# Row-form loads with 28 to 32 KB packets for the output, gate, up and down projections of a decode block on one Trainium2 core

## The chip, the cores and the metric

The kernel is a program for one core of a Trainium2 chip. The metric is device time in microseconds (us). Timed runs of the two kernels alternate on the same chip ("rounds"), and the profiled execution gives a trace. A ratio below is the mean time of one kernel's fast runs over that of the other's of the same rounds, so it is not quite the ratio of the medians that stand beside it; with it comes a 95% interval. The later sessions ran on three different chips (12, 9 and 3 in the record), so a run is compared with the kernel before of its own rounds unless the text says otherwise.

## The reference, cut to what matters

One decode step (sequence length 1) for a batch of 8: adaptive layer norm, grouped-query attention over a long cache, a ReGLU feed-forward block. Everything is bf16.

```python
# x (8,1,1024); k_cache, v_cache (8,4,8192,128): 67 MB each; wq (1024,4096); wo (4096,1024)
# W_gate, W_up (1024,3584); W_down (3584,1024); w_mod (1024,6144)
mod = silu(c) @ w_mod                      # six vectors: sa, ca, ga, sb, cb, gb
h = layernorm(x) * (1 + ca) + sa
x = x + ga * (attention(h @ wq, k_cache, v_cache) @ wo)      # 32 heads, 4 KV heads
h = layernorm(x) * (1 + cb) + sb
x = x + gb * ((relu(h @ W_gate) * (h @ W_up)) @ W_down)
```

185.6 MB are read from HBM once each and used for 8 rows, so the kernel is a stream of loads with computation hung onto it. K and V are 134.2 MB of it, wo 8.4 MB, gate and up 14.7 MB together, W_down 7.3 MB.

## The kernel before

All large loads go through one ring in SBUF, `arena`: nine slots of 8192 bf16 elements per partition. A load is issued by SP, the engine that only issues DMAs, as soon as everything in its target space has been read (`pump`). Loads start in order, and a load of 128 partitions is spread over the core's 16 DMA engines, 8 partitions each: a K or V load lands 4.9 us after the one before it, which is eight packets of 611 ns.

The loads that the change touches. What matters is the contiguous run in HBM that goes to one partition, because it becomes one DMA packet (the trace of the kernel before has 4096 packets of 2 KB for wo): for wo, eight runs of 2 KB per partition and load; for gate and up, 14 KB; for W_down, 14 KB.

```python
wo_src = A_wo.rearrange("(q h d) n -> q d h n", q=4, d=128)      # partition = element d of a head
g_src = B_W_gate.rearrange("(p k) n -> p (k n)", k=KC)
u_src = B_W_up.rearrange("(p k) n -> p (k n)", k=KC)
d_src = B_W_down.rearrange("(q p r) n -> q p (r n)", p=128, r=FR)   # FR = 7
for i in range(4):
    load(("wo", i), wo_src[i], SLOT)
for i in range(4):
    load(("gate", i), g_src[:, i * 2 * F:(i + 1) * 2 * F], 2 * F)
    load(("up", i), u_src[:, i * 2 * F:(i + 1) * 2 * F], 2 * F)
wd_parts = [(q, 0, FR) for q in range(NB - 1)] + [(NB - 1, 0, 4), (NB - 1, 4, 6), (NB - 1, 6, 7)]
for i, (q, r0, r1) in enumerate(wd_parts):
    load(("wd", i), d_src[q][:, r0 * D:r1 * D], (r1 - r0) * D)
```

Attention works on 32 groups (8 batch entries x 4 KV heads). For our argument one part matters: the product of the probabilities with V takes 64 small matmuls per group, each with its own weight load.

```python
def pv(n):
    z = n % 2
    col = n * J
    # ... (vv: V of the group as 64 chunks of 128 keys; pv_: the probabilities, turned)
    for cc in range(NC):                          # NC = 64
        fns.append(lambda e, cc=cc: e.matmul(ps[:, 3, col:col + J], vv[:, cc, :], pv_[:, cc % 16, cc // 16, :],
                                             start=(cc == 0), stop=(cc == NC - 1)))
```

The four projections of the tail: wo with oT (128 elements of a head x 32 heads) as it comes out of attention; gate and up with the weights as the stationary operand, 28 blocks of 128 outputs; W_down column-tiled, four column tiles of 32 each for a quarter of the outputs.

```python
# wo: 32 heads x 4 column tiles, moving 256 columns
ps[32 * j:32 * j + 32, 5, 0:256], oT[:, h, :], w[:, hh, j, :]
# gate, up: per row block kk, 28 matmuls of 8 moving columns, each with a 128x128 weight load
ps[:, 0, off + f * B:off + (f + 1) * B], w[:, f // FR, f % FR, :], hT[:, kk, 0:B]
# ... relu and product on 128x224, written as hmT for W_down
```

Of the kernel before, what the change touches and what calls it, by code (L numbers as in the profile page):

```python
# [132 lines left out]
def bass_adaLN_cond__gqa_block_cached__glu_gated_reglu__decode_kernel(nc, A_x, A_k_cache, A_v_cache, A_wq, A_wo, B_x, B_W_gate, B_W_up, B_W_down, c, w_mod, out):  # L133
# [13 lines left out]
    FR = 7  # L147
    NB = F // (128 * FR)
    KF = NB * FR

    P = Prog()
    with ExitStack() as es:
        E = es.enter_context

        def sb(name, shape, dtype):
            return E(nc.sbuf_tensor(name, shape, dtype))
# [34 lines left out]
        grel = sb("grel", [128, KF, B], dt.float32)  # L191
        hmT = sb("hmT", [128, KF, 32], dt.bfloat16)
# [7 lines left out]
        def R(t, lo=0, hi=1):  # L200
            return (t, lo, hi)
# [4 lines left out]
        def slot_r(lo, hi):  # L206
            return ("arena", lo, hi)
# [5 lines left out]
        def load(key, src, n):  # L213
            stream.append((key, src, n))
# [17 lines left out]
        wo_src = A_wo.rearrange("(q h d) n -> q d h n", q=4, d=128)  # L232
        g_src = B_W_gate.rearrange("(p k) n -> p (k n)", k=KC)
        u_src = B_W_up.rearrange("(p k) n -> p (k n)", k=KC)
        d_src = B_W_down.rearrange("(q p r) n -> q p (r n)", p=128, r=FR)
# [7 lines left out]
        for i in range(4):  # L243
            load(("wo", i), wo_src[i], SLOT)
        for i in range(4):
            load(("gate", i), g_src[:, i * 2 * F:(i + 1) * 2 * F], 2 * F)
            load(("up", i), u_src[:, i * 2 * F:(i + 1) * 2 * F], 2 * F)
        wd_parts = [(q, 0, FR) for q in range(NB - 1)] + [(NB - 1, 0, 4), (NB - 1, 4, 6), (NB - 1, 6, 7)]
        for i, (q, r0, r1) in enumerate(wd_parts):
            load(("wd", i), d_src[q][:, r0 * D:r1 * D], (r1 - r0) * D)  # L250
# [23 lines left out]
        P.op("pool", lambda e: e.memset(hmT[:], 0.0), writes=[R("hmT", 0, KF)])  # L274
# [228 lines left out]
        for q in range(4):  # L503
            w = arena[:, place["wo", q]:place["wo", q] + SLOT].rearrange("p (h j n) -> p h j n", h=8, j=4)
            fns = []
            for hh in range(8):
                for j in range(4):
                    h = 8 * q + hh
                    fns.append(lambda e, w=w, hh=hh, h=h, j=j: e.matmul(  # L509
                        ps[32 * j:32 * j + 32, 5, 0:256], oT[:, h, :], w[:, hh, j, :], start=(h == 0), stop=(h == Hq - 1),  # L510
                        tile_position=(0, 32 * j)))
            P.op("pe", fns, reads=[R("oT"), slot_r(place["wo", q], place["wo", q] + SLOT)], writes=[bank(5)])
# [8 lines left out]
        for i in range(4):  # L521
            gf, uf = [], []
            for kk in (2 * i, 2 * i + 1):
                for fns, base, off in ((gf, place["gate", i], 0), (uf, place["up", i], KF * B)):
                    w = arena[:, base + (kk % 2) * F:base + (kk % 2 + 1) * F].rearrange("p (q x r) -> p q r x", q=NB, r=FR)
                    for f in range(KF):
                        first = kk == 0 and off == 0 and f == 0
                        fns.append(lambda e, w=w, f=f, kk=kk, off=off, first=first: e.matmul(  # L528
                            ps[:, 0, off + f * B:off + (f + 1) * B], w[:, f // FR, f % FR, :], hT[:, kk, 0:B],
                            start=first, stop=(kk == KC - 1), skip_group_check=True))  # L530
            P.op("pe", gf, reads=[R("hT"), slot_r(place["gate", i], place["gate", i] + 2 * F)], writes=[bank(0)])
            P.op("pe", uf, reads=[R("hT"), slot_r(place["up", i], place["up", i] + 2 * F)], writes=[bank(0)])
        P.op("act", lambda e: e.activation(grel[:].rearrange("p f b -> p (f b)"), ps[:, 0, 0:KF * B], ACT.Relu),  # L533
             reads=[bank(0)], writes=[R("grel")])
        P.op("dve", lambda e: e.tensor_tensor(out=hmT[:, :, 0:B], in0=ps[:, 0, KF * B:2 * KF * B].rearrange("p (f b) -> p f b", b=B),  # L535
                                              in1=grel[:], op=ALU.mult),
             reads=[bank(0), R("grel"), R("hmT", 0, KF)], writes=[R("hmT", 0, KF)])
        for i, (q, r0, r1) in enumerate(wd_parts):
            lo, hi = place["wd", i], place["wd", i] + (r1 - r0) * D
            w = arena[:, lo:hi].rearrange("p (r j n) -> p r j n", r=r1 - r0, j=4)  # L540
            fns = []
            for r in range(r0, r1):
                for j in range(4):
                    f = q * FR + r
                    fns.append(lambda e, w=w, r=r - r0, f=f, j=j: e.matmul(  # L545
                        ps[32 * j:32 * j + 32, 1, 0:256], hmT[:, f, :], w[:, r, j, :], start=(f == 0), stop=(f == KF - 1),
                        tile_position=(0, 32 * j)))
            P.op("pe", fns, reads=[R("hmT", 0, KF), slot_r(lo, hi)], writes=[bank(1)])
        P.op("dve", lambda e: e.tensor_tensor(out=lu[:], in0=ps[:, 1, 0:256], in1=mod[:, 5, :], op=ALU.mult),
             reads=[bank(1), R("mod", 5, 6)], writes=[R("lu")])  # L550
# [45 lines left out]
```

## Time and profile before

| | before |
|---|---|
| time, median of 4 runs | 445.77 us (445.73 to 446.13) |
| span of the traced run | 444.1 us |
| bytes read from HBM | 185.63 MB |
| DMA packets | 16,770 |
| PE, DVE busy | 66%, 49% |

The DMA part of the page of the kernel before. The line "DMA" has one digit per fortieth of the span, the mean busy share of the 16 DMA engines in tenths (9 is 90% or more), and "GB/s" what they moved. Queue q1 carries the kernel's loads; q8 and q14 carry instructions to the core's engines.

```profile
DMA  8999999999999999999999999999999999999993
GB/s 344 421 428 425 434 434 428 426 429 437 427 428 432 431 426 426 435 434 425 426 434 429 425 429 435 429 425 432 429 430 428 429 421 403 422 430 429 426 429 151
DMA packets 16770, 186.14 MB, mean 419 GB/s; under 512 B 1537, under 2 KB 1633, under 8 KB 5985
...
q1 hardware_dynamic: 16704, 185.64, 98.5%
q8 instruction: 27, 0.44, 0.4%
...
DMA 83%; PE 8%; DVE 7%; issue 1%; ACT 0%; SPq 0%; POOL 0%; DVEq 0%; ACTq 0%; POOLq 0%
```

The reader should see three things. The DMA engines are busy from the second slice on, and the last line, the chain of work that ended last, is DMA for 83% of its length: the kernel is bound by its stream of loads. There is a dip to 403 GB/s in the slice from 366 to 377 us, which is where wo begins to arrive. And the last slice is at 151 GB/s.

The table of stretches for the tail, kernel before. Columns: stretch in us, its length, busy time (and number of instructions) of PE, PE's weight loads, DVE, ACT and POOL, granted PE clock, DMA share (busy packet time over 16 engines' time), GB/s.

```profile
core 0: us, PE busy (x) PEld busy (x) DVE busy (x) ACT busy (x) POOL busy (x), PEclk, DMA share, GB/s
300.00:366.00 66.00, 48.64 (x566) 26.15 (x565) 40.54 (x60) 5.44 (x14) 4.05 (x20) 0.82 1.01 428
366.00:388.00 22.00, 14.25 (x255) 10.25 (x251) 7.87 (x15) 2.84 (x5) 0.00 (x0) 0.77 1.05 411
388.00:421.00 33.00, 22.97 (x413) 22.20 (x414) 4.33 (x11) 0.20 (x1) 0.00 (x0) 0.53 1.01 429
...
431.00:436.00 5.00, 1.69 (x28) 0.96 (x28) 0.00 (x0) 0.00 (x0) 0.00 (x0) 0.50 0.90 377
436.00:440.00 4.00, 2.97 (x52) 1.52 (x52) 0.00 (x0) 0.00 (x0) 0.00 (x0) 0.50 0.41 167
```

In wo's stretch (366 to 388 us) the DMA share is 1.05. In the last two rows the share falls to 0.90 and 0.41 while loads are still outstanding: some of the 16 engines have finished and others have not.

PE's own waits after 366 us, kernel before, longest first (engine, tile and line; what it waited for; us in total, times, longest):

```profile
PE ps L545 <- DMA arena<-in_B_W_down_dram: 7.4, 5, 2.9
PE ps L528 <- DMA arena<-in_B_W_up_dram: 3.0, 3, 1.4
PE ps L509 <- DMA arena<-in_A_wo_dram: 2.6, 1, 2.6
...
PE ps L528 <- DMA arena<-in_B_W_gate_dram: 2.3, 2, 1.2
```

PE waits 15.3 us for loads in the tail, so work taken from it there cannot shorten the kernel by itself.

The reading of the last two stretches can be made exact. A load's semaphore is incremented once by each of its 16 engines when that engine's share has landed. The skill says the same ("DMA: Bandwidth & Descriptors", "Why a DMA increments its semaphore by 16 and not by 1": only the full 16 means that all data landed), and the trace records the times of the increments. For the last load of W_down in the kernel before (first of the 16 landings at 434.43 us of the span), the others came after it by, in us:

```
0.00 0.11 0.72 0.95 1.23 1.40 1.42 3.12 4.18 4.19 4.54 5.28 5.42 5.59 5.60 5.91
```

The kernel cannot go on before the last of them, at 440.33 us. I call the distance from the first to the last landing of this load the lag; it is 5.9 us here. For the fourth load of wq, at 52 us, it was 1.5 us, and for the last load of w_mod, at 32 us, 1.2 us.

### The profile page before, as it was taken

The page shows a single profiled execution, that of the slowest core. Times are in us where ns is not written, and L with a number is a line of the kernel's source. Part 1 is how long each engine was busy: PE and PEld are TensorE (multiplying, and loading weights), DVE is VectorE, ACT ScalarE, POOL GpSimd, SP SyncE. Part 2 cuts the span into 40 slices and gives each one's busy share as a digit, 9 for nine tenths or more (in the row PEclk, how much of TensorE's full clock was granted, in tenths as well). Part 3 has the DMA queues.
Part 4 walks back from the last instruction along what each step waited for, and adds up shares of the span by engine and source line. Part 5 has one row for each costly group of instructions (what it writes and reads, how often), then busy time and mean ns, then how long its engine had stood idle before and what let it go on. Part 6 is the DMA issues. An engine that isn't in the chain of part 4 may idle for free.

```text
span 444.1 us, 7822 instructions
## 1 busy us (share of the span) xinstructions
PE 290.9 (66%) x3514; PEld 165.4 (37%) x3514; DVE 217.7 (49%) x333; ACT 33.2 (7%) x78; POOL 30.8 (7%) x141
## 2 busy tenths in 40 slices
PE   0235355677858676776877767786777787558753
PEld 0111022344434333443433334343333345348741
DVE  0503065666655566666555566665556664230000
ACT  0200010000001000000100000001000002000000
POOL 4000020100000001000000110000001000000000
PEclk9995576887788888879688888778888869655555
DMA  8999999999999999999999999999999999999993
GB/s 344 421 428 425 434 434 428 426 429 437 427 428 432 431 426 426 435 434 425 426 434 429 425 429 435 429 425 432 429 430 428 429 421 403 422 430 429 426 429 151
DMA packets 16770, 186.14 MB, mean 419 GB/s; under 512 B 1537, under 2 KB 1633, under 8 KB 5985
## 3 DMA queue, kind: packets, MB, share of 16 engines
q1 hardware_dynamic: 16704, 185.64, 98.5%
q8 instruction: 27, 0.44, 0.4%
q14 instruction: 7, 0.05, 0.0%
q10 hardware_dynamic: 32, 0.01, 0.0%
HBM read 185.63 MB, written 0.02 MB: 418 GB/s over the span
## 4 chain that ended last, share of the span: by engine, by line
DMA 83%; PE 8%; DVE 7%; issue 1%; ACT 0%; SPq 0%; POOL 0%; DVEq 0%; ACTq 0%; POOLq 0%
DMA arena<-in_A_k_cache_dram 62%; DMA arena<-in_B_W_down_dram 8%; DMA arena<-in_A_wq_dram 7%; DMA arena<-in_A_wo_dram 4%; PE ps L460 4%; DVE kt L411 3%; DMA c_r<-in_c_dram 2%; PE ps L528 1%; DVE pT L450 1%; PE ps L334 1%; PE ps L420 1%; PE ps L357 0%; DVE lu L281 0%; ACT L278 0%; DVE hT L286 0%
## 5 line engine op out<-in xcount | busy, mean ns | idle before, releaser
L411 DVE STREAM_TRANSPOSE kt<-arena 128x1024 uint32<-128x1024 uint32 x128 | 153.3, 1218 | 114.6 <-DMA arena<-in_A_k_cache_dram 114.6
L420 PE MATMUL ps<-kt,qpad 128*128 128x512 bf16 x512 | 161.5, 482 | 2.0 <-POOL qpad L400 2.0
L420 PEld LDWEIGHTS ps<-kt,qpad 128*128 128x128 bf16 x512 | 60.9, 119 | 91.8 <-issue 60.6
L460 PE MATMUL ps<-pT,arena 128*128 128x8 bf16 x2048 | 56.0, 166 | 49.2 <-DVE pT L450 49.2
L460 PEld LDWEIGHTS ps<-pT,arena 128*128 128x128 bf16 x2048 | 54.1, 96 | 63.6 <-issue 63.3
L400 POOL COPY qpad<-qR 32x32 bf16<-32x32 bf16 x128 | 26.0, 203 | 312.8 <-PE ps L420 256.0
L430 PE MATMUL ps<-identf,negm 128*128 128x128 f32 x64 | 20.2, 408 | 37.0 <-DVE negm L426 37.0
L444 ACT ACTIVATE prb<-ps,bias 128x512 bf16<-128x512 f32 x32 | 22.0, 687 | 283.9 <-DVE mjt L438 283.9
L528 PE MATMUL ps<-hT,arena 128*128 128x8 bf16 x448 | 24.8, 194 | 7.7 <-DMA arena<-in_B_W_up_dram 3.0
L528 PEld LDWEIGHTS ps<-hT,arena 128*128 128x128 bf16 x448 | 24.4, 153 | 8.1 <-DMA arena<-in_B_W_up_dram 3.2
L430 PEld LDWEIGHTS ps<-identf,negm 128*128 128x128 f32 x64 | 12.3, 240 | 40.3 <-DVE negm L426 40.3
L450 DVE STREAM_TRANSPOSE pT<-prb 128x512 bf16<-128x512 bf16 x32 | 21.5, 672 | 1.7 <-ACT prb L444 1.7
L426 DVE TENSOR_REDUCE negm<-ps 128x1 f32<-128x512 f32 x32 | 20.9, 653 | 1.0 <-PE ps L420 1.0
L535 DVE TENSOR_TENSOR hmT<-ps,grel 128x224 bf16<-128x224 f32 x1 | 0.4, 391 | 30.7 <-ACT grel L533 30.7
L357 PE MATMUL ps<-arena,hT 128*32 128x512 bf16 x64 | 7.6, 627 | 11.2 <-DMA arena<-in_A_wq_dram 8.4
L303 PE MATMUL ps<-st,sel 128*128 128x1 f32 x4 | 1.2, 362 | 19.3 <-DVE st L302 19.3
L334 PE MATMUL ps<-arena,hT 128*32 128x512 bf16 x96 | 9.0, 544 | 6.8 <-DMA arena<-in_w_mod_dram 6.8
L545 PE MATMUL ps<-arena,hmT 128*32 128x256 bf16 x112 | 7.1, 415 | 7.4 <-DMA arena<-in_B_W_down_dram 7.4
L509 PE MATMUL ps<-arena,oT 128*32 128x256 bf16 x128 | 6.4, 382 | 5.2 <-DMA arena<-in_A_wo_dram 2.6
L341 DVE COPY mod<-ps 128x512 f32<-128x512 f32 x2 | 1.3, 670 | 15.2 <-PE ps L334 15.2
L436 DVE TENSOR_REDUCE mj<-ps 128x8 f32<-128x128 f32 x32 | 8.1, 252 | 1.2 <-PE ps L430 1.2
L303 PEld LDWEIGHTS ps<-st,sel 128*128 128x128 f32 x4 | 1.0, 310 | 19.6 <-DVE st L302 19.6
(64 smaller groups left out, 66.0 us busy)
## 6 DMA issues: line engine op xcount, KB each, us to landing
arena<-in_A_k_cache_dram SPq DMA_DIRECT2D x32, 2048.0 KB, 25.7
arena<-in_A_v_cache_dram SPq DMA_DIRECT2D x32, 2048.0 KB, 30.2
arena<-in_w_mod_dram SPq DMA_DIRECT2D x4, 3072.0 KB, 18.2
arena<-in_A_wq_dram SPq DMA_DIRECT2D x4, 2048.0 KB, 35.0
arena<-in_A_wo_dram SPq DMA_DIRECT2D x4, 2048.0 KB, 19.1
arena<-in_B_W_gate_dram SPq DMA_DIRECT2D x4, 1792.0 KB, 24.2
arena<-in_B_W_up_dram SPq DMA_DIRECT2D x4, 1792.0 KB, 28.0
arena<-in_B_W_down_dram SPq DMA_DIRECT2D x3, 1792.0 KB, 33.8
```

What stands on the lines that cost most here:

```text
L334: fns.append(lambda e, w=w, pr=pr, j=j, kk=kk: e.matmul(ps[32 * j:32 * j + 32, pr, :], hT[:, kk, :], w[:, 2 * pr:2 * pr + 2, j, :], start= ...
L357: fns.append(lambda e, w=w, z=z, g=g, kk=kk: e.matmul(ps[32 * g:32 * g + 32, 3 + z, :], hT[:, kk, :], w[:, g, z, :], start=(kk == 0), stop ...
L400: P.op("pool", lambda e, n=n, Q=Q: e.tensor_copy(qpad[32 * Q:32 * Q + 32, n % NQ, :, 24 + 32 * Q:32 + 32 * Q], qR[32 * Q:32 * Q + 32, :, n ...
L411: P.op("dve", lambda e: e.transpose(ktb[:, to:to + QE].bitcast(dt.uint32), arena[:, lo:lo + QE].bitcast(dt.uint32)), reads=[slot_r(lo, lo ...
L420: fns.append(lambda e, t=t, r=r: e.matmul(ps[:, n % 2, :].rearrange("p (c k) -> p c k", k=32), qpad[:, n % NQ, t * 2 + r, 24 - 8 * i:152 - ...
L426: P.op("dve", lambda e: e.tensor_reduce(negm[:, n % 2:n % 2 + 1], ps[:, n % 2, :], AX.X, ALU.max, negate=True), reads=[bank(n % 2)], write ...
L430: P.op("pe", lambda e: e.matmul(ps[:, 2, 0:128], negm[:, n % 2:n % 2 + 1].to_broadcast([128, 128]), identf[:], start=True, stop=True), rea ...
L436: P.op("dve", lambda e: e.tensor_reduce(mj[:, z, :], ps[:, 2, 0:128].rearrange("p (m j) -> p j m", j=J), AX.X, ALU.min), reads=[bank(2)], ...
L444: P.op("act", lambda e: e.activation(prb[:, z, :], ps[:, z, :], ACT.Exp, bias=bias[:, z:z + 1], scale=scale, accum_out=lall[:, n:n + 1]), ...
L450: P.op("dve", lambda e: e.transpose(pT[:, z, :], prb[:, z, :]), reads=[R("prb", z, z + 1)], writes=[R("pT", z, z + 1)])
L460: fns.append(lambda e, cc=cc: e.matmul(ps[:, 3, col:col + J], vv[:, cc, :], pv_[:, cc % 16, cc // 16, :], start=(cc == 0), stop=(cc == NC ...
L528: fns.append(lambda e, w=w, f=f, kk=kk, off=off, first=first: e.matmul(ps[:, 0, off + f * B:off + (f + 1) * B], w[:, f // FR, f % FR, :], ...
```

## The change

Its intent is to give every weight of the tail the form "partition p holds consecutive rows", so that each partition receives long contiguous runs: wo in two loads of 32 KB per partition instead of four with 2 KB runs, gate and up in two loads each of 28 KB, W_down in parts of 28, 14, 8, 4 and 2 KB. For that the activations need the matching row order, which costs work: the heads are turned into rows by 32 small matmuls with an identity, two evacuations and one DVE transpose. Gate and up swap their operands: activations become stationary, weights move, and four column tiles work side by side (the Trainium skill's "TensorEngine Tiling (Array Packing)", "When to Use Tiling", names this "Stationary-Streaming Swap + Column Tiling"). That leaves 128 matmuls where there were 448.

```diff
-        wo_src = A_wo.rearrange("(q h d) n -> q d h n", q=4, d=128)
+        wo_src = A_wo.rearrange("(p k) n -> p (k n)", k=KO)
-        d_src = B_W_down.rearrange("(q p r) n -> q p (r n)", p=128, r=FR)
+        d_src = B_W_down.rearrange("(p k) n -> p (k n)", k=KF)
-        for i in range(4):
-            load(("wo", i), wo_src[i], SLOT)
 ...
+        wo_parts = [(0, 16), (16, 32)]
+        for i, (r0, r1) in enumerate(wo_parts):
+            load(("wo", i), wo_src[:, r0 * D:r1 * D], (r1 - r0) * D)
+        gu_parts = [(0, 4), (4, 8)]
+        for i, (r0, r1) in enumerate(gu_parts):
+            load(("gate", i), g_src[:, r0 * F:r1 * F], (r1 - r0) * F)
+            load(("up", i), u_src[:, r0 * F:r1 * F], (r1 - r0) * F)
+        wd_parts = [(0, 14), (14, 21), (21, 25), (25, 27), (27, 28)]
 ...
+        for z in range(2):                       # heads into rows
+            for jj in range(4):
+                for g in range(G):
+                    ... e.matmul(ps[32 * g:32 * g + 32, z, 128 * jj:128 * jj + 128], oT[:, J * g + 4 * z + jj, :], identb[:], ...
 ...
+        P.op("dve", lambda e: e.transpose(oX, orow... .rearrange("p (x k) -> p k x", k=KO)), ...
 ...
-                            ps[:, 0, off + f * B:off + (f + 1) * B], w[:, f // FR, f % FR, :], hT[:, kk, 0:B],
+                                ps[32 * j:32 * j + 32, b0 + h, 0:H], hT[:, kk, :], w[:, r, j, h, :],
+                                start=(kk == 0), stop=(kk == KC - 1), tile_position=(0, 32 * j)))
 ...
+        P.op("dve", lambda e: e.transpose(hmT, hrow.rearrange("p (x k) -> p k x", k=KF)), ...
```

Some small tiles move into space of the K buffer that is free by then.

More of the change, by code (lines that the diff above doesn't have):

```diff
@@ L146, in bass_adaLN_cond__gqa_block_cached__glu_gated_reglu__decode_kernel @@
     NSLOT = 9
-    FR = 7
-    NB = F // (128 * FR)
-    KF = NB * FR
+    KF = F // 128
+    KO = Hq * Dh // 128
+    FJ = F // 4
     P = Prog()
@@ L190, in bass_adaLN_cond__gqa_block_cached__glu_gated_reglu__decode_kernel @@
         oT = sb("oT", [128, Hq, 32], dt.bfloat16)
-        grel = sb("grel", [128, KF, B], dt.float32)
-        hmT = sb("hmT", [128, KF, 32], dt.bfloat16)
+        orow = ktb[:, 0:1024].rearrange("p (j d) -> p j d", j=J)
+        oX = ktb[:, 1024:2048].rearrange("p (k b) -> p k b", b=32)
+        hrow = ktb[:, 2048:2048 + FJ]
+        hmT = ktb[:, 3072:3072 + FJ].rearrange("p (k b) -> p k b", b=32)
+        grel = ktb[:, 4096:4096 + 2 * FJ].bitcast(dt.float32)
+        r_oX, r_hmT = ("kt", 1024, 2048), ("kt", 3072, 4096)
         ob = sb("ob", [128, 256], dt.bfloat16)
@@ L242, in bass_adaLN_cond__gqa_block_cached__glu_gated_reglu__decode_kernel @@
             load(("v", n), A_v_cache[n // G, n % G].rearrange("(p c) d -> p (c d)", p=128), SLOT)
-        for i in range(4):
-            load(("wo", i), wo_src[i], SLOT)
-        for i in range(4):
-            load(("gate", i), g_src[:, i * 2 * F:(i + 1) * 2 * F], 2 * F)
-            load(("up", i), u_src[:, i * 2 * F:(i + 1) * 2 * F], 2 * F)
-        wd_parts = [(q, 0, FR) for q in range(NB - 1)] + [(NB - 1, 0, 4), (NB - 1, 4, 6), (NB - 1, 6, 7)]
-        for i, (q, r0, r1) in enumerate(wd_parts):
-            load(("wd", i), d_src[q][:, r0 * D:r1 * D], (r1 - r0) * D)
+        wo_parts = [(0, 16), (16, 32)]
[6 more added lines that the diff above has]
+        wd_parts = [(0, 14), (14, 21), (21, 25), (25, 27), (27, 28)]
+        for i, (r0, r1) in enumerate(wd_parts):
+            load(("wd", i), d_src[:, r0 * D:r1 * D], (r1 - r0) * D)
         P.op("pool", lambda e: e.memset(c_r[:], 0.0), writes=[R("c_r", 0, 4)])
@@ L273, in bass_adaLN_cond__gqa_block_cached__glu_gated_reglu__decode_kernel @@
         P.op("pool", lambda e: e.memset(oT[:], 0.0), writes=[R("oT")])
-        P.op("pool", lambda e: e.memset(hmT[:], 0.0), writes=[R("hmT", 0, KF)])
         P.op("pool", lambda e: e.tensor_copy(identb[:], identf[:]), reads=[R("identf")], writes=[R("identb")])
@@ L500, in bass_adaLN_cond__gqa_block_cached__glu_gated_reglu__decode_kernel @@
              reads=[bank(3), R("lx"), R("oT")], writes=[R("oT")])
-        for q in range(4):
-            w = arena[:, place["wo", q]:place["wo", q] + SLOT].rearrange("p (h j n) -> p h j n", h=8, j=4)
+        for z in range(2):
             fns = []
-            for hh in range(8):
+            for jj in range(4):
+                for g in range(G):
+                    fns.append(lambda e, z=z, jj=jj, g=g: e.matmul(
+                        ps[32 * g:32 * g + 32, z, 128 * jj:128 * jj + 128], oT[:, J * g + 4 * z + jj, :], identb[:],
+                        start=True, stop=True, tile_position=(0, 32 * g)))
+            P.op("pe", fns, reads=[R("oT"), R("identb")], writes=[bank(z)])
+            dst = orow[:, 4 * z:4 * z + 4, :].rearrange("p j d -> p (j d)")
+            if z == 0:
+                P.op("dve", lambda e, dst=dst, z=z: e.tensor_copy(dst, ps[:, z, :]), reads=[bank(z)], writes=[("kt", 512 * z, 512 * z + 512)])
+            else:
+                P.op("act", lambda e, dst=dst, z=z: e.activation(dst, ps[:, z, :], ACT.Copy), reads=[bank(z)],
+                     writes=[("kt", 512 * z, 512 * z + 512)])
+        P.op("dve", lambda e: e.transpose(oX, orow.rearrange("p j d -> p (j d)").rearrange("p (x k) -> p k x", k=KO)),
+             reads=[("kt", 0, 1024)], writes=[r_oX])
+        for i, (r0, r1) in enumerate(wo_parts):
+            lo, hi = place["wo", i], place["wo", i] + (r1 - r0) * D
+            w = arena[:, lo:hi].rearrange("p (r j n) -> p r j n", r=r1 - r0, j=4)
+            fns = []
+            for k in range(r0, r1):
                 for j in range(4):
-                    h = 8 * q + hh
-                    fns.append(lambda e, w=w, hh=hh, h=h, j=j: e.matmul(
-                        ps[32 * j:32 * j + 32, 5, 0:256], oT[:, h, :], w[:, hh, j, :], start=(h == 0), stop=(h == Hq - 1),
+                    fns.append(lambda e, w=w, r=k - r0, k=k, j=j: e.matmul(
+                        ps[32 * j:32 * j + 32, 5, 0:256], oX[:, k, :], w[:, r, j, :], start=(k == 0), stop=(k == KO - 1),
                         tile_position=(0, 32 * j)))
-            P.op("pe", fns, reads=[R("oT"), slot_r(place["wo", q], place["wo", q] + SLOT)], writes=[bank(5)])
+            P.op("pe", fns, reads=[r_oX, slot_r(lo, hi)], writes=[bank(5)])
         P.op("dve", lambda e: e.tensor_tensor(out=lu[:], in0=ps[:, 5, 0:256], in1=mod[:, 2, :], op=ALU.mult),
@@ L518, in bass_adaLN_cond__gqa_block_cached__glu_gated_reglu__decode_kernel @@
         modulate(4, 3)
-        for i in range(4):
-            gf, uf = [], []
-            for kk in (2 * i, 2 * i + 1):
-                for fns, base, off in ((gf, place["gate", i], 0), (uf, place["up", i], KF * B)):
-                    w = arena[:, base + (kk % 2) * F:base + (kk % 2 + 1) * F].rearrange("p (q x r) -> p q r x", q=NB, r=FR)
-                    for f in range(KF):
-                        first = kk == 0 and off == 0 and f == 0
-                        fns.append(lambda e, w=w, f=f, kk=kk, off=off, first=first: e.matmul(
-                            ps[:, 0, off + f * B:off + (f + 1) * B], w[:, f // FR, f % FR, :], hT[:, kk, 0:B],
-                            start=first, stop=(kk == KC - 1), skip_group_check=True))
-            P.op("pe", gf, reads=[R("hT"), slot_r(place["gate", i], place["gate", i] + 2 * F)], writes=[bank(0)])
-            P.op("pe", uf, reads=[R("hT"), slot_r(place["up", i], place["up", i] + 2 * F)], writes=[bank(0)])
@@ L533, in bass_adaLN_cond__gqa_block_cached__glu_gated_reglu__decode_kernel @@
-        P.op("act", lambda e: e.activation(grel[:].rearrange("p f b -> p (f b)"), ps[:, 0, 0:KF * B], ACT.Relu),
-             reads=[bank(0)], writes=[R("grel")])
-        P.op("dve", lambda e: e.tensor_tensor(out=hmT[:, :, 0:B], in0=ps[:, 0, KF * B:2 * KF * B].rearrange("p (f b) -> p f b", b=B),
-                                              in1=grel[:], op=ALU.mult),
-             reads=[bank(0), R("grel"), R("hmT", 0, KF)], writes=[R("hmT", 0, KF)])
-        for i, (q, r0, r1) in enumerate(wd_parts):
+        H = FJ // 2
@@ new lines, in bass_adaLN_cond__gqa_block_cached__glu_gated_reglu__decode_kernel @@
+        for i, (r0, r1) in enumerate(gu_parts):
+            for nm, b0 in (("gate", 0), ("up", 2)):
+                lo, hi = place[nm, i], place[nm, i] + (r1 - r0) * F
+                w = arena[:, lo:hi].rearrange("p (r j h n) -> p r j h n", r=r1 - r0, j=4, h=2)
+                fns = []
+                for kk in range(r0, r1):
+                    for h in range(2):
+                        for j in range(4):
+                            fns.append(lambda e, w=w, r=kk - r0, kk=kk, h=h, j=j, b0=b0: e.matmul(
+                                ps[32 * j:32 * j + 32, b0 + h, 0:H], hT[:, kk, :], w[:, r, j, h, :],
+                                start=(kk == 0), stop=(kk == KC - 1), tile_position=(0, 32 * j)))
+                P.op("pe", fns, reads=[R("hT"), slot_r(lo, hi)], writes=[bank(b0, 2)])
@@ new lines, in bass_adaLN_cond__gqa_block_cached__glu_gated_reglu__decode_kernel @@
+        for h in range(2):
+            P.op("act", lambda e, h=h: e.activation(grel[:, H * h:H * h + H], ps[:, h, 0:H], ACT.Relu), reads=[bank(h)],
+                 writes=[("kt", 4096 + FJ * h, 4096 + FJ * h + FJ)])
+            P.op("dve", lambda e, h=h: e.tensor_tensor(out=hrow[:, H * h:H * h + H], in0=ps[:, 2 + h, 0:H],
+                                                       in1=grel[:, H * h:H * h + H], op=ALU.mult),
+                 reads=[bank(2 + h), ("kt", 4096 + FJ * h, 4096 + FJ * h + FJ)], writes=[("kt", 2048 + H * h, 2048 + H * h + H)])
@@ L539, in bass_adaLN_cond__gqa_block_cached__glu_gated_reglu__decode_kernel @@
+        P.op("dve", lambda e: e.transpose(hmT, hrow.rearrange("p (x k) -> p k x", k=KF)), reads=[("kt", 2048, 2048 + FJ)],
+             writes=[r_hmT])
+        for i, (r0, r1) in enumerate(wd_parts):
             lo, hi = place["wd", i], place["wd", i] + (r1 - r0) * D
@@ L541, in bass_adaLN_cond__gqa_block_cached__glu_gated_reglu__decode_kernel @@
             fns = []
-            for r in range(r0, r1):
+            for k in range(r0, r1):
                 for j in range(4):
-                    f = q * FR + r
-                    fns.append(lambda e, w=w, r=r - r0, f=f, j=j: e.matmul(
-                        ps[32 * j:32 * j + 32, 1, 0:256], hmT[:, f, :], w[:, r, j, :], start=(f == 0), stop=(f == KF - 1),
+                    fns.append(lambda e, w=w, r=k - r0, k=k, j=j: e.matmul(
+                        ps[32 * j:32 * j + 32, 4, 0:256], hmT[:, k, :], w[:, r, j, :], start=(k == 0), stop=(k == KF - 1),
                         tile_position=(0, 32 * j)))
-            P.op("pe", fns, reads=[R("hmT", 0, KF), slot_r(lo, hi)], writes=[bank(1)])
-        P.op("dve", lambda e: e.tensor_tensor(out=lu[:], in0=ps[:, 1, 0:256], in1=mod[:, 5, :], op=ALU.mult),
-             reads=[bank(1), R("mod", 5, 6)], writes=[R("lu")])
+            P.op("pe", fns, reads=[r_hmT, slot_r(lo, hi)], writes=[bank(4)])
+        P.op("dve", lambda e: e.tensor_tensor(out=lu[:], in0=ps[:, 4, 0:256], in1=mod[:, 5, :], op=ALU.mult),
+             reads=[bank(4), R("mod", 5, 6)], writes=[R("lu")])
         P.op("dve", lambda e: e.tensor_tensor(out=ob[:], in0=lu[:], in1=x1[:], op=ALU.add),
```

## The prediction

> **What bounds the kernel now.** The DMA engines. The chain of waits is DMA for 83% of its length; in the table of stretches the DMA share is 0.98 or more from 4 to 431 us. PE is busy 66%, DVE 49%. SP waits for space in the ring of buffers, but a load takes 25 to 36 us from issue to landing, so some five are always queued. After 360 us PE waits for data: 7.4 us for W_down, 5.3 us for gate and up, 2.6 us for wo. PE work saved there is off the path.
>
> **What a byte costs.** The trace's packet records took, by size (median): 2 KB 84 ns, 4 KB 159, 8 KB 309, 14 KB 535, 16 KB 611, 24 KB 912: 75 ns per 2 KB plus 9 to 12 ns per packet. The Trainium skill ("DMA: Bandwidth & Descriptors", "Why small descriptors are slow (HBM only)") states a fixed cost per packet; this trace agrees. So 28 KB should take 1061 ns and 32 KB 1211 ns (estimates from that line).
>
> **What the change does to the stream** (same bytes, 16 engines):
> - wo: 4096 packets of 2 KB x 84 ns / 16 = 21.5 us (its loads landed over 21.3 us) become 256 of 32 KB: 19.4 us. Saves 1.9 us.
> - gate and up: 1024 of 14 KB, 34.2 us, become 512 of 28 KB, 33.9 us. Saves 0.3 us.
> - W_down: saves 0.1 us. The end after the last landing (3.8 us) stays.
> - The 16 landings of one load spread over 1.2 us early, 6.0 us at the end: single engines fall back when a 16 KB instruction packet comes among theirs. Seven such fall after 366 us. The tail's PE instructions go from 1376 to 800, two or three fetches fewer: 0 to 0.6 us on the slowest engine.
>
> **What it adds**, on PE, DVE and ACT: between oT (380.6 us) and wo, 32 matmuls, two evacuations of 0.7 us, one strided transpose of 128x1024, estimated 2.3 us from hT's 0.62 us for 256: some 4.5 us. wo's products then end near 392 us, not 389.8, and hT comes near 399, not 396. Gate and up become 128 column-tiled matmuls, 3 us per 3.67 MB instead of 3.1 us per 1.8 MB. ReLU, product and transpose add about 4 us after the last up load.
> None of it should reach the path. Bigger loads need bigger space, later: gate1 is issued when wo0 is read (about 389 us), up1 at 392, W_down at 402, while the queue holds data until 403, 412 and 420 us. hmT is ready near 428 us, the first W_down part lands near 429.
>
> **Predicted**: 445.8 - 2.3 - 0.3 = 443.2 us; 442.2 to 444.7 holds it 8 times in 10. Faster by over 2%: 0.02; within 2%: 0.96; slower by over 2%: 0.02.
>
> **What would show it.** Right: wo's stretch from about 405 to about 430 GB/s; packets of 28 and 32 KB near 1061 and 1211 ns; some 12,000 packets, not 16,770; the chain still ends in DMA of W_down; PE busy less, without effect. Wrong: DMA share under 0.9 between 366 and 430 us (ring starved), PE last before the output, or more ns per byte.
>
> **What would make it wrong.** A ring that starves while PE turns heads (slower by some us); big packets colliding in HBM; instruction fetches stuck behind big packets.

## The result, and the profile after

| | before | after |
|---|---|---|
| time, median | 445.77 us (445.73 to 446.13, 4 runs) | 445.15 us (444.3 to 445.5, 4 runs) |
| ratio | | 0.9982 (0.9964 to 0.9999) |
| span of the traced run | 444.1 us | 443.4 us |
| DMA packets | 16,770 | 12,175 |
| instruction packets on q8 | 27 | 25 |

A gain of 0.6 us and not 2.6: the same within 2%, as predicted, but outside the stated range of 442.2 to 444.7 us. Where did two microseconds go?

The same lines of the page after:

```profile
DMA  9999999999999999999999999999999999999992
GB/s 356 410 430 426 430 433 435 426 426 432 432 430 429 427 430 430 432 430 429 429 427 433 429 429 427 435 430 430 426 432 429 433 437 430 428 441 421 445 409 119
DMA packets 12175, 186.11 MB, mean 420 GB/s; under 512 B 1424, under 2 KB 1520, under 8 KB 1776
...
q1 hardware_dynamic: 12112, 185.64, 98.1%
q8 instruction: 25, 0.41, 0.3%
...
DMA 79%; PE 10%; DVE 8%; issue 1%; ACT 1%; SPq 0%; POOL 0%; DVEq 0%; ACTq 0%; POOLq 0%
```

and the same stretches after:

```profile
300.00:366.00 66.00, 49.65 (x549) 26.11 (x548) 40.04 (x58) 5.14 (x14) 4.05 (x20) 0.81 1.01 431
366.00:388.00 22.00, 13.50 (x269) 9.94 (x270) 10.91 (x17) 3.44 (x6) 0.00 (x0) 0.74 1.00 430
388.00:421.00 33.00, 13.71 (x176) 6.81 (x168) 4.32 (x11) 1.18 (x3) 0.00 (x0) 0.66 1.00 431
...
431.00:436.00 5.00, 2.26 (x48) 1.39 (x40) 0.00 (x0) 0.00 (x0) 0.00 (x0) 0.50 0.76 311
436.00:440.00 4.00, 3.23 (x52) 1.24 (x44) 0.00 (x0) 0.00 (x0) 0.00 (x0) 0.50 0.18 73
```

The dip at wo is gone (411 to 430 GB/s), and the DMA share there went from 1.05 to 1.00. The ring never starves: the share is 1.00 up to 421 us. But look at the end. From 436 to 440 us the engines now move 73 GB/s instead of 167: **more of them have finished early, and the kernel waits for the few that have not.** The mean rate gained where the change was made; the finish did not follow.

PE's waits after 366 us, kernel after:

```profile
PE ps L553 <- DMA arena<-in_B_W_up_dram: 8.9, 2, 5.3
PE ps L571 <- DMA arena<-in_B_W_down_dram: 8.8, 4, 5.3
PE ps L553 <- DMA arena<-in_B_W_gate_dram: 5.3, 1, 5.3
```

Now it waits 23.0 us for loads: PE's saving became waiting, as the prediction said. Nothing new stands at the end either: from the last landing to the end of the span it is 3.80 us in both traces.

The landings say it in numbers. "Packets" are those of q8, the instructions of PE (that they are PE's is shown by the experiments: PE instructions added or removed change their number, by one per 256). Lag and landings are of the last W_down load.

| trace | q8 packets | first landing | last landing | lag |
|---|---|---|---|---|
| before | 27 | 434.43 | 440.33 | 5.90 |
| after | 25 | 433.18 | 439.56 | 6.38 |

The first engine to finish gained 1.25 us. The last one gained 0.77 us, because the lag grew by 0.48. Neither is the 2.3 us of the prediction.

Why does the last engine lag? The packet records of the trace of the kernel after, around 433.4 us, where one of the five q8 packets of the tail stands (columns: start us, end us, queue, bytes, duration ns; lines of other engines left out):

```
432.853 433.388  q1 14336  535
433.385 434.264  q8 16384  879      <- instructions for PE
434.248 434.273  q1     4   25
434.259 435.105  q1  8192  846      <- the packet behind it; 309 ns for all others of its size
```

One instruction packet holds one DMA engine for 879 ns, and the load packet behind it takes 537 ns longer than its kind: 1.42 us in all, on one engine out of 16. This is the rule in every trace: of the 27 q8 packets of the kernel before, the 24 whose follower could be identified cost 1.43 us in the median (1.42 to 1.55); of the 25 of the kernel after, 1.43 us as well. Here it met one of the two engines that were last already: the last landing of W_down's first part came 4.96 us after its first landing, that of the second part 6.57 us after. Sorted by lag, the other 15 landings of the two parts differ by 0.05 us at most. So between the two loads one engine alone fell back, and the packet at 433.4 us is the only one in that time.

The traces also hint at who carries these packets. The durations of the q8 packets repeat with a period of eight: in after_p60 (below) the last sixteen took 879, 886, 941, 933, 928, 960, 967, 949 and then 879, 879, 941, 933, 928, 960, 964, 955 ns. In all fourteen traces a packet differs from the eighth after it by 1 to 7 ns in the median, from the next one by 11 to 33. That is what eight engines in turn look like. The records do not name the engine, so it is a strong hint and not a proof.

### The profile page after: what moved, and what is told of

Read it like the earlier page. It is cut to its first block, busy times and chain, and to the rows that moved or that the text cites. A ratio compares the mean times of both kernels' runs of the same rounds, so it can differ in the third digit from the quotient of the medians.

```text
span 443.4 us, 7249 instructions
## 1 busy us (share of the span) xinstructions
PE 282.4 (64%) x3226; PEld 147.4 (33%) x3226; DVE 222.7 (50%) x337; ACT 34.4 (8%) x80; POOL 30.0 (7%) x140
## 2 busy tenths in 40 slices
DMA packets 12175, 186.11 MB, mean 420 GB/s; under 512 B 1424, under 2 KB 1520, under 8 KB 1776
## 4 chain that ended last, share of the span: by engine, by line
DMA 79%; PE 10%; DVE 8%; issue 1%; ACT 1%; SPq 0%; POOL 0%; DVEq 0%; ACTq 0%; POOLq 0%
DMA arena<-in_A_k_cache_dram 62%; DMA arena<-in_B_W_down_dram 8%; DMA arena<-in_A_wq_dram 7%; PE ps L465 4%; DVE kt L416 3%; DMA c_r<-in_c_dram 2%; DVE pT L455 2%; PE ps L532 1%; PE ps L425 1%; PE ps L553 1%; PE ps L339 1%; PE ps L362 0%; DVE kt L522 0%; DVE lx L501 0%; DVE lu L286 0%
## 5 line engine op out<-in xcount | busy, mean ns | idle before, releaser
L425 PE MATMUL ps<-kt,qpad 128*128 128x512 bf16 x512 | 163.9, 488 | 2.0 <-POOL qpad L405 2.0
L553 PE MATMUL ps<-arena,hT 128*32 128x448 bf16 x128 | 12.7, 577 | 16.6 <-DMA arena<-in_B_W_up_dram 8.9
L560 DVE TENSOR_TENSOR kt<-ps,kt 128x448 bf16<-128x448 f32 x2 | 1.2, 620 | 27.1 <-PE ps L553 27.1
L571 PE MATMUL ps<-arena,kt 128*32 128x256 bf16 x112 | 6.9, 416 | 8.8 <-DMA arena<-in_B_W_down_dram 8.8
L553 PEld LDWEIGHTS ps<-arena,hT 128*32 128x32 bf16 x128 | 4.5, 139 | 24.1 <-DMA arena<-in_B_W_up_dram 10.5
L532 PE MATMUL ps<-arena,kt 128*32 128x256 bf16 x128 | 6.3, 389 | 2.7 <-DVE kt L522 2.7
```

The lines of the kernel that those rows point to most:

```text
L425: fns.append(lambda e, t=t, r=r: e.matmul(ps[:, n % 2, :].rearrange("p (c k) -> p c k", k=32), qpad[:, n % NQ, t * 2 + r, 24 - 8 * i:152 - ...
L532: fns.append(lambda e, w=w, r=k - r0, k=k, j=j: e.matmul(ps[32 * j:32 * j + 32, 5, 0:256], oX[:, k, :], w[:, r, j, :], start=(k == 0), sto ...
L553: fns.append(lambda e, w=w, r=kk - r0, kk=kk, h=h, j=j, b0=b0: e.matmul(ps[32 * j:32 * j + 32, b0 + h, 0:H], hT[:, kk, :], w[:, r, j, h, : ...
```

## The experiments

**Theory 1.** The end is set by the slowest of the 16 DMA engines. The stream of loads is the same for all; what makes an engine slow is how many PE instruction packets it had to carry, 1.43 us each. They go to eight of the engines in turn, so what counts is not the number of packets but the most that one engine gets: four for 25 to 32 packets, three for 17 to 24. The change cut the packets from 27 to 25, which is still four on the worst engine.

**Theory 2.** The new form of W_down (28 KB packets, rows 57 KB apart) is itself slower by the 1.2 us that its stretch lost between the last landings (17.3 us before, 18.5 us after).

**Theory 3.** A fetch costs its bytes, shared by all 16 engines, about 0.1 us; the finish is an accident of one run.

All twelve runs gave the right result (the padded kernels too: their extra matmuls write to space that is not read). The edit that removes PE instructions appears in five runs and needs a word. It packs the product with V: one matmul takes four chunks of 128 keys at once (32 stationary columns, 4 x 8, against 512 moving columns, 4 x 128), four column tiles side by side; only the blocks in which both chunk numbers agree are wanted, and they are summed by four matmuls with a 0/1 selector after a copy on ACT. A group then takes 20 matmuls instead of 64, each with its weight load: 88 instructions fewer. It touches no load.

### The changed kernel again (after_again)

No edit.

> The changed kernel once more, for a second trace of it. Theory 1 (the end is set by the slowest of the 16 DMA engines, and an engine is slow by the number of 16 KB PE instruction packets it had to carry, 1.4 us each, handed to 8 engines in turn): 25 such packets, the worst engine carries 4, first landing of the last W_down load near 433.2 us of the span, last landing 6.0 to 6.6 us after it, time 444.3 to 445.5 us. Theory 2 (W_down in 28 KB packets from rows 57 KB apart is itself slower): all 16 engines late in W_down's stretch, the first landing too. Theory 3 (the 1.2 us lost in W_down was an accident of one run): last landing 5 us or less after the first, time near 443.8 us.

Measured: 445.31 us (444.47 to 445.52), ratio to before 0.9967 (0.9954 to 0.9980); before was 446.66 us in these rounds. 25 packets, first landing 433.02, last 439.71, lag 6.69 us. So the lag is no accident of one run, and the first landing is not late: theory 2 and the accident in theory 3 both lose ground. The traces settle theory 2: from the first landing of up's last load to that of W_down's last load it is 17.09 us in the kernel before and 17.09 and 17.07 us in the two traces of the changed kernel. W_down's own loads did not get slower.

The times have two clusters. In this and the later rounds most runs of the kernel before are at 445.7 to 446.0 or at 446.5 to 446.9 us. The changed kernel has them too: of its nine runs in both sessions three are at 444.3 to 444.5 and six at 445.1 to 445.5 us. In the first session all four runs of the kernel before were in their faster cluster (445.7 to 446.1), three of the four runs of the changed kernel in their slower one. Cluster against cluster the change gains about 1.3 us; this is taken up below.

### 264 PE instructions fewer (after_k3)

```diff
-                pv(n - 1)
+                (pv_packed if n - 1 < 3 else pv)(n - 1)
```

with `pv_packed` as described, for 3 of 32 groups (in the kernel the 3 is a constant, PACK; the buffers and the summing matmuls are left out here).

> The changed kernel with the attention product of 3 of the 32 groups in fewer PE instructions (264 fewer): same loads, same packets, 24 PE instruction packets and not 25, so that none comes in the W_down stretch as the fourth of its engine. Theory 1: worst engine carries 3, last landing 1.4 us earlier, lag of the slowest engine about 4.9 us instead of 6.4, time 443.7 us (443.2 to 444.1). Theory 2: no change against the changed kernel, 445.1 us. Theory 3, and any view in which a fetch costs its bytes shared by 16 engines: 0.1 us less, 445.0 us.

Measured: 444.03 us (443.73 to 444.13), ratio to before 0.9943 (0.9931 to 0.9955), so 1.28 us under the changed kernel of the same rounds. 24 packets on q8:

```profile
q8 instruction: 24, 0.39, 0.3%
```

First landing 433.02 us, as before the edit; last 438.50, lag 5.48 us. One instruction packet fewer out of 25, 0.01% of the bytes, is worth 1.3 us in the medians and 1.2 us between the last landings of the two traces; by theory 1, since it was a fourth one on an engine that was last. Two of the five runs of the changed kernel were in its faster cluster (444.5 us), and against those the gain is only 0.45 us. The first landing did not move, so the gain does not come from a PE that frees buffers sooner. Theories 2 and 3 expected nothing or 0.1 us. The time was 0.3 us above the middle of what theory 1 expected, since the lag was 5.5 and not 4.9 us.

### 1536 PE instructions more (after_p24)

```diff
             make_qpad(n + 2)
+            P.op("pe", [lambda e: e.matmul(ps[0:8, 7, 8:9], identb[:, 0:8], identb[:, 0:1], start=True, stop=True)] * 24,
+                 reads=[R("identb")], writes=[bank(7)])
```

> The changed kernel with 24 extra tiny matmuls after each of the 32 groups (1536 more PE instructions, result unused): 31 PE instruction packets. Theory 1: 8 engines take turns, 25 to 32 packets are 4 on the worst engine, so six more packets cost nothing at the end: 445.1 us, within 0.4. A view in which every packet costs 1.4 us of the whole stream: plus 8 us. A view in which its cost is shared by 16 engines: plus 0.5 us, 445.7 us. If PE became the bound (it should not, it idles 3 us per group): slower by more, and PE would be seen busy in the stretches.

Measured: 445.45 us (445.37 to 445.74), 0.14 us over the changed kernel of the same rounds; 31 packets, first landing 432.95, last 439.79, lag 6.84 us. PE was busy 69% instead of 64%, still far from the bound. Six packets more cost next to nothing, one packet fewer gained 1.3 us. In the medians no smooth cost per packet does both; a count of the most on one engine does. (Against the two faster runs of the changed kernel this run costs 1.0 us, so the times alone would not exclude a smooth cost of some 0.2 us a packet; the landings do. Here seven of the eight late engines landed 5.8 to 6.8 us after the first and one at 4.3, as seven fours and one three would have it.)

### 2176 PE instructions more (after_p34)

The same with 34 instead of 24.

> The same with 34 extra tiny matmuls per group (2176 more PE instructions): 33 or 34 PE instruction packets, so the first engine of the eight carries a fifth. Theory 1: plus 1.4 us against the changed kernel and against the run with 24 extra matmuls: 446.5 us (446.0 to 447.0), lag of the slowest engine near 7.8 us. Theory 2 and theory 3: plus 0.1 to 0.7 us at most, and no step between 24 and 34 extra matmuls.

Measured: 445.94 us (445.86 to 446.82), 0.63 us over the changed kernel, 0.49 over the run with 24. 34 packets, lag 7.18 us. Direction right, size a miss: 1.4 us was expected. The landings show why. Of the last load, eight engines landed 5.64, 5.80, 5.82, 5.89, 6.06, 6.40, 6.83 and 7.18 us after the first, the other eight within 3.27 us. Four packets are 4 x 1.43 = 5.72 us, and on top of that each engine carries something of its own, 0 to 1.2 us, from early in the run. The 33rd packet (at 418.2 us) gave a fifth one to an engine that was some 5.8 us behind, not the latest, and made it the last, by 0.4 us; the 34th (at 438.7 us) came too late to matter. That eight engines stand apart from the other eight is the picture that theory 1 wants.

### 3840 PE instructions more (after_p60)

The same with 60.

> The changed kernel with 60 extra tiny matmuls per group (3840 more PE instructions): 40 PE instruction packets, five on each of eight engines. With 34 extra ones only two engines had a fifth and the last landing moved 0.4 us, since those two were not the ones that were late already. Theory 1: now the latest engine has a fifth too, so its lag is 6.8 + 1.4 = 8.2 us, last landing near 441.2 us, time 446.6 to 447.2 us; eight engines between 7.1 and 8.3 us, the other eight under 3.5. Shared-bytes view: 1.3 us over the changed kernel with all 16 engines equally late.

Measured: 446.84 us (446.70 to 446.99), ratio to before 1.0009 (0.9991 to 1.0027). 40 packets, first landing 433.13, last 441.38, lag 8.25 us. Eight engines landed 6.89 to 8.25 us after the first, the others within 3.24 us. Fifteen packets more than in the changed kernel came from 3840 instructions: 256 each. The Trainium skill ("Runtime: NRT & Kernel Launch", "Instruction fetch mechanics") states just this block, 16 KiB or 256 instructions, so the count agrees. It also calls the cost of crossing a block "mostly hidden". Here it is not hidden: it is taken from one engine of a stream that has no slack.

### The output projection alone (wo_row)

The kernel before with the new form of wo and the turning of heads; gate, up and down as before.

```diff
-        wo_src = A_wo.rearrange("(q h d) n -> q d h n", q=4, d=128)
+        wo_src = A_wo.rearrange("(p k) n -> p (k n)", k=KO)
-        for i in range(4):
-            load(("wo", i), wo_src[i], SLOT)
+        wo_parts = [(0, 16), (16, 32)]
 ... (and the turning of heads)
```

> The kernel before with the output projection alone changed (rows, two loads of 32 KB packets, heads turned); gate, up and down as before. If 2 KB packets really cost 84 ns each, the first landing of the last load (an engine that no PE instruction packet visits) comes 2.1 us earlier than in the kernel before (434.4 us of the span); if they overlap, as the landings of the unvisited engine say (20.5 us for wo and not 21.5), 1.2 us earlier: 433.2 us, and nearly the whole gain of the change on such an engine is here. PE instructions 64 more than before, 28 instruction packets, the worst engine carries 4 as before: lag 5.9 to 6.8 us, time 0.8 to 1.4 us under the kernel before, like the changed kernel.

Measured: 445.29 us (444.49 to 445.79) beside 446.26 us for before, ratio 0.9974 (0.9956 to 0.9991). First landing 433.16 us, 1.27 us before that of the kernel before; 28 packets, lag 6.09 us. So on an engine that carries no instructions wo is worth 1.27 us, not 2.1: the durations of 2 KB packets, 84 ns each, cannot be added up, because the records overlap by some 4 ns. The spacing of the first landings over wo's four loads was 20.51 us, or 80 ns for each of an engine's 256 packets; in 32 KB packets (in the changed kernel) 19.33 us, or 75.5 ns per 2 KB.

This run also showed, by chance, how little PE matters: its traced execution had a mean granted PE clock of 0.552 instead of 0.77, and its span was the second shortest up to then.

```profile
core 0: 443.0 us, clock 0.552
```

### All but the output projection (after_wo_old)

The changed kernel with wo's loads and product as before.

> The changed kernel with the output projection as before (four loads of 2 KB packets, no turning of heads); gate, up and down in the new form. Stream on an unvisited engine: first landing of the last load 434.2 us, 0.2 us under the kernel before. 25 PE instruction packets, 4 on the worst engine: time within 0.5 us of the kernel before. Theory 2 (the new form of W_down is slower by 1.2 us): about 1 us slower than the kernel before, and first landing 435 us or later.

Measured: 445.53 us (445.41 to 446.31), ratio to before 0.9984 (0.9967 to 1.0002). First landing 434.12 us, 0.31 us under before; 25 packets, lag 5.76 us. This ends theory 2: with the new W_down and, as before, four packets on the worst engine, the stream is faster, not slower. The two parts add up: 1.27 + 0.31 = 1.58 us, against 1.25 and 1.41 us in the two traces of the whole change.

### 880 PE instructions fewer, without the change (before_k10)

The kernel before with `pv_packed` for 10 groups.

> The kernel before with the attention product of 10 of the 32 groups in fewer PE instructions (880 fewer): 24 PE instruction packets and not 27, loads and packets untouched. Theory 1: the worst engine carries 3 and not 4, first landing of the last load still 434.4 us, lag 4.5 to 5.1 us and not 5.9, time 0.9 to 1.4 us under the kernel before. A view in which fetches cost only their shared bytes: 0.3 us less. No part of the change under study is in it.

Measured: 445.32 us (445.23 to 445.41), ratio 0.9976 (0.9961 to 0.9991), 0.94 us under the median of before in the same rounds, but only 0.45 us under its faster cluster. 24 packets, first landing 434.42 us as before, lag 5.30 us where 4.5 to 5.1 was expected. The direction holds without any part of the change, but the size was smaller than a full packet: the last engine had a larger lag of its own. This engine-to-engine offset of about 1 us is real and not explained. It is there before the first instruction packet (at 37 to 43 us): at w_mod's last load (32 us) the lag was 0.8 to 1.4 us in all fourteen traces. At wq's last load (52 us), after that packet, it was 1.5 to 1.9 us in nine traces and 2.2 to 2.9 us in five, depending on whether the packet met an engine that lagged already.

### 2816 PE instructions fewer, with the change and without it (after_k32, after_k32_b, before_k32)

`pv_packed` for all 32 groups.

> The changed kernel with all 32 groups' attention product in fewer PE instructions (2816 fewer): 14 PE instruction packets, at most 2 per engine. Theory 1: first landing unchanged at 433.0 us, lag of the slowest engine 3.4 to 4.0 us (2 x 1.42 and some 0.9 of other lag), last landing near 436.8 us, time 441.9 to 443.0 us, 2.5 to 3 us under the changed kernel. Shared-bytes view: 1.0 us under it. If PE or ACT got in the way (one copy of 0.6 us more per group on ACT) the chain of waits would name it; not expected.

> The kernel before with all 32 groups' attention product in fewer PE instructions (2816 fewer): 16 PE instruction packets, at most 2 on an engine, as in the changed kernel with the same edit (14). With the packets per engine equal, the two differ by the stream alone: this one 1.3 us slower than the changed kernel with the edit (that one 442.5 us in the session before), so 443.8 us, 443.3 to 444.2. First landing 434.4 us, lag 3.4 to 4.0 us.

> The changed kernel with all 32 groups' attention product in fewer PE instructions, again, beside the kernel before with the same edit: 442.5 us, within 0.4, 3.3 to 4.2 us under the kernel before of the same rounds; lag of the slowest engine 3.4 to 4.0 us.

Measured:

| kernel | time | ratio to before | q8 packets | first landing | last landing | lag |
|---|---|---|---|---|---|---|
| after_k32 | 442.46 us (442.40 to 442.70) | 0.9913 (0.9897 to 0.9928) | 14 | 433.01 | 436.87 | 3.86 |
| after_k32_b | 442.51 us (441.84 to 442.72) | 0.9913 (0.9894 to 0.9933) | 14 | 432.98 | 436.25 | 3.27 |
| before_k32 | 443.90 us (443.81 to 443.94) | 0.9943 (0.9925 to 0.9960) | 16 | 434.39 | 438.22 | 3.83 |

The last two ran in the same rounds. With two packets on the worst engine in both, the change is worth 443.90 - 442.51 = 1.39 us, which is what the first landings say (434.39 - 432.98 = 1.41). That is the change's value where the packets weigh equally; in the first comparison 0.62 us of it arrived. Packing the product with V is worth more: 446.54 to 443.90 us in the kernel before (medians of the same rounds), or 1.8 us from its faster cluster. The version with both beats both kernels.

Its tail in the table of stretches, for comparison with the two above:

```profile
366.00:388.00 22.00, 13.73 (x151) 7.37 (x155) 9.65 (x16) 4.84 (x9) 0.00 (x0) 0.66 1.01 435
...
431.00:436.00 5.00, 2.35 (x56) 1.06 (x45) 0.00 (x0) 0.00 (x0) 0.00 (x0) 0.84 0.72 291
436.00:440.00 4.00, 1.02 (x12) 0.25 (x12) 0.85 (x2) 0.00 (x0) 0.00 (x0) 0.50 0.03 7
```

In the last stretch the DMA share is 0.03 and DVE is already at the final sums: the loads are over.

### The kernel before again (before_again)

No edit.

> The kernel before once more, for a second trace of it, since its time was 445.8 us in one session and 446.3 to 446.7 in others. Theory 1: the stream of an unvisited DMA engine is the same in every trace (first landing of the last load 434.4 us), 27 PE instruction packets, 4 on the worst engine, last landing 5.9 to 6.9 us after the first: the two times differ by where an engine starts from, not by the stream.

Measured: 445.87 us (445.76 to 448.41), the other kernel before of the same rounds 446.54 us (445.68 to 447.88), ratio 1.0000 (0.9978 to 1.0023). 27 packets, first landing 434.37 us, last 440.17, lag 5.80 us. The stream repeats to 0.06 us between the two traces. Both traces fell in the faster cluster of times, so what happens in a run of 446.7 us was not seen; the larger gain of the change in the later rounds (ratio 0.9967, against 0.9982 at first) comes from the kernel before being in its slower cluster more often there. The record has a hint. The kernels whose packets divide evenly over eight engines (24 in after_k3 and before_k10, 40 in after_p60, 16 in before_k32) keep within 0.4 us over their runs. Those in which some engines carry one more (25, 27, 28 and 34 packets) spread over 0.9 us or more. (31 and 14 packets do not fit so neatly: 0.4 us in after_p24, 0.3 us in after_k32, but 0.9 us in after_k32_b.) That would fit an odd packet that meets an engine with a large offset in one run and with a small one in the next. It is not shown: no trace of the kernel before fell in its slower cluster, none of the changed kernel in its faster one.

## Why the prediction was right or wrong

Right:

- The bound. DMA stayed the bound; PE busy fell from 22.97 to 13.71 us in the gate and up stretch without effect.
- The ring. Nothing starved. The issue of the second gate load was predicted for 389 us and came at 388.6, the second up load 392 and 391.3, W_down 402 and 400.6. hmT was ready at 427.3 us (predicted 428), W_down's first part landed at 429.53 (429).
- The packets. 28 KB took 1062 ns (1061 predicted), 32 KB 1213 ns (1211), and there were 12,175 packets (some 12,000). The records of 2 to 32 KB fit 75.3 ns per 2 KB plus a fixed 8 to 9 ns; that there is a fixed cost agrees with the Trainium skill ("DMA: Bandwidth & Descriptors", "Why small descriptors are slow (HBM only)").

Wrong, in two terms of the sum "445.8 - 2.3 - 0.3":

- **"wo: ... Saves 1.9 us"**, the main part of the 2.3. It took 4096 packets times 84 ns over 16 engines, and found this confirmed by loads that "landed over 21.3 us". Both numbers were too large for the stream. Packet records overlap: at 2 KB they are 80 ns apart and not 84, which the DMA share of 1.05 in wo's stretch said in the profile of before. And 21.3 us was the spacing of the last landings, in which the last engine also fell back by an instruction packet; the first landings were 20.5 us apart. Measured by itself, wo saves 1.27 us. Gate, up and down together saved 0.31 us where 0.4 was predicted. The stream as a whole gained 1.25 to 1.58 us, not 2.3.
- **"two or three fetches fewer: 0 to 0.6 us on the slowest engine"**. Two fewer it was (27 to 25). But the term treated fetches as an amount that shrinks evenly. They are whole steps of 1.43 us on one engine, given to eight engines, and the finish follows the engine with most. 27 and 25 both leave four on the worst engine. In the traces the lag went up, by 0.48 us at first, instead of down. By how much it went up is luck: the traced run before was of the faster cluster, the traced run after of the slower one.

Together: 1.25 - 0.48 = 0.77 us earlier in the traces, 0.6 us in the medians of the same session. With cluster against cluster it would have been about 1.3 us, so bad luck has a share in the miss, but 2.6 us was out of reach. The decisive evidence for the second term is in the landings: one of sixteen fell back at the packet at 433.4 us, and eight fall further back as packets are added (4.2 to 6.4 us with 25, 6.9 to 8.3 us with 40) while the other eight stay within 3.3 us. The medians go the same way: one packet fewer gained 1.28 us (after_k3), six more cost 0.14 us (after_p24) and fifteen more 1.5 us (after_p60, 446.84 against 445.31 in earlier rounds on another chip), while the first landing stayed between 432.95 and 433.18 us in all these kernels.

What is shown and what is not: shown are the cost per fetch, that PE's instruction count sets their number, that eight engines bear them, and, in the landings, the steps. That they go in strict rotation is inferred from the counts and from the period of eight in their durations. The engine-to-engine offset of about 1 us, there from the first loads on, is not explained. That it makes the two clusters of both kernels is likely but not shown.

## What to carry to other kernels

When a kernel is bound by its loads, its end is the last of 16 DMA engines, not their mean: read the landings of the last load one by one before costing a change in bytes or packets. Instructions are loads too: a fully unrolled kernel pays 1.43 us of one DMA engine for every 256 PE instructions here, so fewer, larger matmuls can save time even on an engine that is two thirds busy and off the critical path. And take the cost of small packets from the spacing of landings on an undisturbed engine, never from the sum of packet durations when that sum exceeds the time.

## What the Trainium skill lacked or had wrong

- "Runtime: NRT & Kernel Launch", "Instruction fetch mechanics": it calls the cost of a 16 KiB block boundary mostly hidden. In this kernel, whose DMA engines are always busy, each PE block cost 1.43 us on one of the 16 engines in the median (878 to 1082 ns for itself, 275 to 574 ns on the packet behind it), and one block fewer made the kernel 1.28 us faster in the medians. The block size of 256 instructions agreed (3840 more instructions, 15 more packets).
- "Runtime: NRT & Kernel Launch" does not say on which DMA engines the blocks arrive. Here eight of the 16 bore all of PE's: with 40 packets eight engines landed 6.9 to 8.3 us behind the first, the other eight within 3.3 us.
- "DMA: Bandwidth & Descriptors", "Rules for kernel authors": it gives rules for the size of a transfer, but none for judging a stream by its slowest engine. The lag between the first and the last engine was 5.9 us of 444 in the kernel before and 3.3 to 3.9 us with 14 instruction packets.
- "DMA: Bandwidth & Descriptors", "Why small descriptors are slow (HBM only)": it gives a fixed cost per packet in cycles, but not how it shows in a trace. Records of 2 KB packets lasted 84 ns and came 80 ns apart; in 32 KB packets 2 KB took 75.5 ns. So 2 KB packets cost 6% more than 32 KB packets, where the durations suggest 11%.
